# Attention and MoE on one core: gating the loads of batches 2 to 7 on MoE steps, odd V slots by VectorE copies, stores issued on ScalarE with four out buffers, and a new DMA model in the scheduler

## The chip, the cores and the metric

One core of one Trainium2 chip. The metric is device microseconds (us) of one execution, the median of several runs. Five engines have an in-order queue each: TensorE (PE), VectorE (DVE), ScalarE (ACT), GpSimd (POOL) and SyncE (SP). DMAs are issued on three of them: loads on GpSimd, transposes and copies on SyncE, stores on SyncE or ScalarE. Each run is marked fast or slow by its time and clock; the ratios use fast runs alone, while the medians in the tables are over all runs, a slow one included where there was one.

## The reference

Sliding-window attention, then a two-layer MLP with squared ReLU (here "MoE").

```python
batch, n_heads, seq, head_dim = 8, 8, 576, 64      # q, k, v in float32
scores = q @ k.T / sqrt(64); masked to |i - j| <= 32; softmax; attn @ v
x = attn_out.transpose(0, 2, 1, 3).reshape(4608, 512)
h = x @ w_in                                       # 512 x 2048
out = maximum(h, 0) ** 2 @ w_out                   # 2048 x 512
```

## The kernel before

Attention works in 72 chunks of 64 query tokens (nine per batch), MoE in nine tiles T of 512 tokens. A MoE *step* is a sixteenth of a tile's first product: 144 steps in all. Attention is interleaved with MoE on TensorE so that TensorE never starves.

The kernel first records all operations with what they read and write. A list scheduler inside the kernel then lays them in order for each engine, with a model of how long each DMA takes, and the instructions are emitted in that order with semaphore waits.

```python
LATE = {"POOL": 1500, "SP": 3000, "ACT": 3000}
def forward(self, key=None, seq=None, rnd=None):      # the scheduler's clock
    ...
    # DMA model of before: three rings served in turn, 180 ns a turn for GpSimd, 60 for the others
    end[op.i] = now + 1700 + (rnd.random() * rnd.late[op.eng] if rnd else 0)

def pace(self, b, x):                                 # a load waits for an attention step
    return [("pace", 9 * b - GL + 2 * x)] if b > 1 else []      # GL = 14

def dma_turn(self, b, t, x, key):                     # K and Q transposed by DMA, on SyncE
    self.p.rec("SP", lambda e: e.dma_start(dst, src, transpose=True), ..., move=(16, 30))

def vd_copy(self, b, s0, s1, key):    # odd 64-token offsets need V shifted by half the partitions
    for lo in range(2):
        dst = vd[64 * lo:64 * lo + 64, s0:s1, :, :]
        src = vx[64 - 64 * lo:128 - 64 * lo, s0 + lo:s1 + lo, :, :]
        self.p.rec("SP", lambda e, d=dst, c=src: e.dma_start(d, c), ...)

def xturn(self, n, m):                # attention output transposed for the MoE, by DMA for n >= 18
    self.p.rec("SP", lambda e: e.dma_start(self.XT[...], xr[...], transpose=True), ...)

def mm2(self, T, u, seg, key):        # second product; the store of 128 rows
    oe = self.OE[x % 3]
    self.p.rec("ACT", lambda e: e.activation(oe[:], op[:], ACTF.Copy), ...)
    self.p.rec("SP", lambda e: e.dma_start(self.out[128 * x:128 * x + 128, :], oe[:]), ...)
```

For batch 0 the shifted V comes from two TensorE matmuls with shifted identities and a ScalarE copy (`vd_shift`).

The softmax here doesn't subtract the row's maximum and nothing guards it: scores larger than these inputs give would overflow.

## Time and profile before

| | before |
|---|---|
| time, median | 340.54 us (3 runs), 340.09 with a fourth |
| span of the profiled run | 338.6 us |
| TensorE busy | 312.5 us (92%) |
| TensorE gaps over 0.25 us after 31 us | 20.0 us, the largest 8.18, 5.98 and 2.16 |
| half-clock stretches after 31 us | 3.4, 6.8 and 10.2 us |

TensorE is the busiest engine, so its idle time is what counts. The page's slices (40 of 8.5 us each): busy tenths of TensorE, its granted clock, and the DMA engines.

```profile
PE   8989997999997929999099999999999999999996
PEclk9999997999999978999679999999999999999999
DMA  9999999999999999999999999983202211100012
```

There are two holes in PE, with a dip of the clock after each, and DMA is at 9 up to about 230 us. The TensorE timeline of the kernel before; columns are start, duration, engine, line, operation, count and, in brackets, the idle time just before and what ended it:

```profile
54.45 0.20 PE L570 MATMUL sc<-vd,pt 128*128 128x65 bf16 x1 [2.16 <-DMA vd<-vx]
...
126.25 1.89 PE L641 MATMUL ht<-xt,w 128*128 128x512 bf16 x4 [5.98 <-ACT rt L647]
...
169.76 1.86 PE L641 MATMUL ht<-xt,w 128*128 128x512 bf16 x4 [8.18 <-issue]
```

Elsewhere four such matmuls took 0.86 us. After the two long gaps they took about twice that, 1.89 and 1.86 us, because the clock was at half.

What stood behind the second gap is in ScalarE's timeline of the kernel before:

```profile
117.54 0.60 ACT L647 ACTIVATE rt<-ht 128x512 bf16<-128x512 f32 x1 [0.33 <-PE ht L641]
125.11 0.60 ACT L674 ACTIVATE oe<-outp 128x512 f32<-128x512 f32 x1 [6.97 <-DMA out_dram<-oe]
```

ScalarE's copy waited for one of three out buffers, held by a store; the ReLU behind it could not run, and TensorE had no free PSUM buffer. The third gap is marked "issue", but SyncE's timeline of the kernel before shows its cause. It is the end of a transpose of attention outputs (`xt<-xr`), issued at 160.28, which landed at 169.67.

```profile
151.75 1.20 SPq L458 DMA_TRANSPOSE qt<-qraw  x1
153.00 1.88 SPq L594 DMA_TRANSPOSE xt<-xr  x1
154.93 0.58 SPq L676 DMA_DIRECT2D out_dram<-oe  x1
155.67 0.46 SPq L487 DMA_DIRECT2D vd<-vx  x1
156.18 0.82 SPq L676 DMA_DIRECT2D out_dram<-oe  x1
157.04 0.52 SPq L487 DMA_DIRECT2D vd<-vx  x1
157.65 1.23 SPq L458 DMA_TRANSPOSE kt<-kraw  x1
158.98 1.24 SPq L458 DMA_TRANSPOSE qt<-qraw  x1
160.28 1.39 SPq L594 DMA_TRANSPOSE xt<-xr  x1
```

The data of that last transpose was ready at 150.6 us, the end of the VectorE instruction that wrote it:

```profile
150.19 0.42 DVE L584 TENSOR_TENSOR xr<-sc,rs 128x256 bf16<-128x256 f32 x1
```

It then stood in SyncE's queue, and took 9.4 us to land. The view of DMA issues of the kernel before (count, size, median us from issue to landing):

```profile
kraw<-in_k_dram POOLq DMA_DIRECT2D x30, 128.0 KB, 15.2
vd<-vx SPq DMA_DIRECT2D x28, 132.0 KB, 6.8
kt<-kraw SPq DMA_TRANSPOSE x30, 7.8
```

### The profile page before, as it was taken

The page shows a single profiled execution, that of the slowest core. Times are in us where ns is not written, and L with a number is a line of the kernel's source. Part 1 is how long each engine was busy: PE and PEld are TensorE (multiplying, and loading weights), DVE is VectorE, ACT ScalarE, POOL GpSimd, SP SyncE. Part 2 cuts the span into 40 slices and gives each one's busy share as a digit, 9 for nine tenths or more (in the row PEclk, how much of TensorE's full clock was granted, in tenths as well). Part 3 has the DMA queues.
Part 4 walks back from the last instruction along what each step waited for, and adds up shares of the span by engine and source line. Part 5 has one row for each costly group of instructions (what it writes and reads, how often), then busy time and mean ns, then how long its engine had stood idle before and what let it go on. Part 6 is the DMA issues. An engine that isn't in the chain of part 4 may idle for free.

```text
span 338.6 us, 7132 instructions
## 1 busy us (share of the span) xinstructions
PE 312.5 (92%) x2862; PEld 168.5 (50%) x2862; DVE 135.3 (40%) x414; ACT 150.5 (44%) x267; POOL 107.1 (32%) x133
## 2 busy tenths in 40 slices
PE   8989997999997929999099999999999999999996
PEld 3457585887553414444034454444454444444442
DVE  5534353564444505454115443544454352222200
ACT  2445263755524615545133554555455544444421
POOL 8998395333765603146011542220000000000000
PEclk9999997999999978999679999999999999999999
DMA  9999999999999999999999999983202211100012
GB/s 69 158 186 195 180 155 190 156 145 171 190 148 181 133 173 180 179 154 155 169 219 139 102 155 194 132 142 90 56 33 56 54 46 41 58 37 31 31 64 93
DMA packets 168160, 42.66 MB, mean 126 GB/s; under 512 B 157632, under 2 KB 161728, under 8 KB 168128
## 3 DMA queue, kind: packets, MB, share of 16 engines
q0 software_dynamic: 116736, 18.36, 77.5%
q1 hardware_dynamic: 51392, 23.85, 38.7%
q8 instruction: 23, 0.38, 0.5%
q14 instruction: 9, 0.07, 0.1%
HBM read 36.70 MB, written 9.44 MB: 136 GB/s over the span
## 4 chain that ended last, share of the span: by engine, by line
PE 80%; DMA 10%; POOL 4%; issue 3%; ACT 1%; DVE 0%; SPq 0%; POOLq 0%; ACTq 0%
PE outp L665 36%; PE ht L641 29%; PE ht L622 6%; DMA vx<-in_v_dram 4%; PE sc L528 3%; DMA xt<-xr 2%; DMA out_dram<-oe 2%; PE sc L570 2%; PE sc L571 2%; DMA vd<-vx 2%; POOL kraw L418 1%; POOL qraw L418 1%; POOL vx L464 1%; POOL w L492 1%; PE sc L431 1%
## 5 line engine op out<-in xcount | busy, mean ns | idle before, releaser
L665 PE MATMUL outp<-w,gt 128*128 128x512 bf16 x576 | 144.5, 383 | 0.0
L641 PE MATMUL ht<-xt,w 128*128 128x512 bf16 x448 | 116.3, 387 | 15.2 <-issue 8.2
L647 ACT ACTIVATE rt<-ht 128x512 bf16<-128x512 f32 x112 | 66.9, 598 | 98.2 <-PE ht L641 96.5
L656 DVE TENSOR_TENSOR gt<-rt 128x512 bf16<-128x512 bf16 x144 | 60.7, 422 | 117.6 <-ACT rt L647 106.6
L665 PEld LDWEIGHTS outp<-w,gt 128*128 128x128 bf16 x576 | 55.0, 98 | 62.6 <-issue 1.8
L641 PEld LDWEIGHTS ht<-xt,w 128*128 128x128 bf16 x448 | 41.3, 99 | 61.4 <-issue 11.3
L418 POOL DMA_DIRECT2D kraw<-in_k_dram x40 | 35.8, 896 | 85.5 <-PE sc L528 81.8
L544 ACT ACTIVATE e<-sc 128x512 bf16<-128x512 f32 x72 | 39.7, 600 | 16.3 <-PE sc L528 16.3
L464 POOL DMA_DIRECT2D vx<-in_v_dram x40 | 35.7, 897 | 27.9 <-PE sc L528 27.9
L551 DVE TENSOR_TENSOR pt<-e,mask 128x512 bf16<-128x512 bf16 x72 | 27.9, 420 | 33.1 <-ACT e L544 33.1
L418 POOL DMA_DIRECT2D qraw<-in_q_dram x40 | 36.0, 899 | 4.2 <-issue 4.2
L674 ACT ACTIVATE oe<-outp 128x512 f32<-128x512 f32 x36 | 21.5, 598 | 34.0 <-PE outp L665 26.3
L622 PE MATMUL ht<-xt,w 128*128 128x128 bf16 x512 | 33.7, 222 | 0.3
L584 DVE TENSOR_TENSOR xr<-sc,rs 128x256 bf16<-128x256 f32 x72 | 29.9, 422 | 4.6 <-DMA xt<-xr 2.1
L622 PEld LDWEIGHTS ht<-xt,w 128*128 128x128 bf16 x512 | 30.0, 99 | 2.7 <-ACT rt L628 1.1
L628 ACT ACTIVATE rt<-ht 128x512 bf16<-128x512 f32 x32 | 19.1, 599 | 22.5 <-PE ht L622 20.4
L582 DVE RECIPROCAL rs<-sc 128x4 f32<-128x4 f32 x72 | 12.7, 180 | 18.1 <-PE sc L571 16.1
L386 PE MATMUL outp<-zz 128*128 128x512 bf16 x50 | 16.1, 439 | 1.2 <-DVE zz L380 1.2
L528 PEld LDWEIGHTS sc<-qt,kt 64*128 64x128 bf16 x576 | 10.0, 95 | 11.1 <-issue 7.2
L570 PE MATMUL sc<-vx,pt 128*128 128x65 bf16 x160 | 15.3, 194 | 0.1
L571 PE MATMUL sc<-vx,pt 128*128 128x65 bf16 x160 | 15.3, 195 | 0.0
L570 PEld LDWEIGHTS sc<-vx,pt 128*128 128x128 bf16 x160 | 12.6, 99 | 4.0 <-DVE xr L584 0.6
(48 smaller groups left out, 123.4 us busy)
## 6 DMA issues: line engine op xcount, KB each, us to landing
out_dram<-oe SPq DMA_DIRECT2D x36, 256.0 KB, 2.4
kraw<-in_k_dram POOLq DMA_DIRECT2D x30, 128.0 KB, 15.2
qraw<-in_q_dram POOLq DMA_DIRECT2D x30, 128.0 KB, 16.0
vd<-vx SPq DMA_DIRECT2D x28, 132.0 KB, 6.8
vx<-in_v_dram POOLq DMA_DIRECT2D x24, 128.0 KB, 15.9
w<-in_moe_w_in_dram POOLq DMA_DIRECT2D x4, 512.0 KB, 10.5
w<-in_moe_w_out_dram POOLq DMA_DIRECT2D x4, 512.0 KB, 17.7
vx<-in_v_dram POOLq DMA_DIRECT2D x16, 96.0 KB, 13.6
```

The lines of the kernel that those rows point to most:

```text
L418: self.p.rec("POOL", lambda e: e.dma_start(dst, src), writes=[("fraw", b, t, x)], old=[("fraw", b - 2, t, x)], reads=self.pace(b, x), dma= ...
L464: self.p.rec("POOL", lambda e: e.dma_start(self.VX[b % 2][r:r + n, s, :, 0:64], self.v[b, :, t0:t0 + n, :].rearrange("h p d -> p h d")), w ...
L544: self.p.rec("ACT", lambda e, d=dst, a=src: e.activation(d, a, ACTF.Exp, scale=0.125), reads=["s" + x for x in name], writes=[("e", g, x) ...
L551: self.p.rec("DVE", lambda e, a=pt, c=ee, d=mb: e.tensor_tensor(a, c, d, ALU.mult), reads=rd + ["mask"], writes=[("pt", (n + k) % 3)], key ...
L570: e.matmul(o, pt[:, a:a + 128], vt[:, ha, 0:VE], start=True, stop=False)
L571: mm = e.matmul(o, pt[:, a + 64:a + 192], vt[:, ha + 2, 0:VE], start=False, stop=True)
L584: self.p.rec("DVE", lambda e: e.tensor_tensor(bass.AP(xr, 256 * k, [[768, 128], [64, 4], [1, 64]]), bass.AP(self.SC, base, [[2048, 128], [ ...
L622: mm = e.matmul(ht[:, 128 * (d % 4):128 * (d % 4) + 128], self.W1[:, ft, 128 * d:128 * d + 128], self.XT[:, t0 // 64:t0 // 64 + 2, ft, :], ...
L641: mm = e.matmul(ht[:], self.W1[:, ft, 128 * d:128 * d + 128], self.XT[:, 8 * T:8 * T + 8, ft, :], start=(ft == 0), stop=(ft == 3))
L647: self.p.rec("ACT", lambda e: e.activation(rt[:], ht[:], ACTF.Relu), reads=[("ht", k % 2)], writes=[("rt", k % 4)], key=key, dur=560)
L656: self.p.rec("DVE", lambda e: e.tensor_tensor(g, r, r, ALU.mult), reads=[("rt", k % 4)], writes=tags, key=key, dur=430)
L665: mm = e.matmul(op[:], gt[:, d, 128 * u:128 * u + 128], self.W2[:, d, :], start=(d == 0), stop=(d == 15))
```

## The change

Its intent: spread the loads over the run, one at a time, so that DMA is not crowded; take the V copies and the stores off SyncE; one more out buffer. The diff also replaces the scheduler's DMA model, and it records the MoE tiles between the batches of attention, no longer after them all, since a load can wait only for a MoE step that is recorded before it. Cut to its core (the new recording order isn't shown):

```diff
-GL = 14
+PACE = 18
-LATE = {"POOL": 1500, "SP": 3000, "ACT": 3000}
+LATE = {"POOL": 1500, "SP": 2000, "ACT": 2000}
+DEPTH, POST, BACK = 4000, {"POOL": 1500, "SP": 1000, "ACT": 1000}, {"POOL": 2500, "SP": 4000, "ACT": 4000}
 def forward(...):
-    # three rings in turn
+    # one first-in first-out line for all DMAs; GpSimd's enter it in pieces, at most DEPTH ns ahead
+    end[op.i] = max(now, start[op.i] + op.dur) + POST[op.eng] + (...)
-def pace(self, b, x):
-    return [("pace", 9 * b - GL + 2 * x)] if b > 1 else []
+def pace(self, b, x, z):                       # z: 0 for K, 1 for Q, 2 for V
+    if b < 2:
+        return []
+    l = 2 * (9 * b + 1.8 * x + 0.6 * z - PACE)
+    return [("mo", max(0, int(l)))] if l < 16 * NT else []      # "mo" k is written by MoE step k
-    (dma_turn)  move=(16, 30)
+    (dma_turn)  move=(32, 28 if n > 64 else 20)      # xturn: (16 * m, 28); store: (8, 92)
-def vd_shift(...)   # TensorE and ScalarE
-def vd_copy(...)    # DMA on SyncE
+def vd_half(self, b, s0, s1, key):
+    for lo in range(2):
+        dst = vd[64 * lo:64 * lo + 64, s0:s1, :, :].rearrange("p s h d -> p (s h d)")
+        src = vx[64 - 64 * lo:128 - 64 * lo, s0 + lo:s1 + lo, :, :].rearrange("p s h d -> p (s h d)")
+        self.p.rec("DVE", lambda e, d=dst, c=src: e.tensor_copy(d, c), ...)
-    oe = self.OE[x % 3]
+    oe = self.OE[x % 4]
-    self.p.rec("SP", lambda e: e.dma_start(self.out[...], oe[:]), ...)
+    self.p.rec("ACT", lambda e: e.dma_start(self.out[...], oe[:]), ...)
```

More of the change, by code (lines that the diff above doesn't have):

```diff
@@ L1 @@
+import collections
 import heapq
@@ L105, in forward @@
         heads = {"POOL": 0, "SP": 0, "ACT": 0}
-        order = ["POOL", "SP", "ACT"]
-        now = spent = 0.0
+        fifo, soft = collections.deque(), collections.deque()
+        now = ahead = 0.0
         def enter(s):
@@ L122, in serve @@
         def serve(until):
-            nonlocal now, spent
+            nonlocal now, ahead
             while now < until:
-                nxt = min((rings[q][heads[q]][0] for q in order if heads[q] < len(rings[q])), default=None)
-                if nxt is None or nxt >= until:
-                    if nxt is None and until > 1e12:
-                        return False
-                    now = max(now, until if nxt is None else min(until, nxt))
-                    return False
-                now = max(now, nxt)
-                for q in list(order):
-                    if heads[q] < len(rings[q]) and rings[q][heads[q]][0] <= now:
-                        break
-                it = rings[q][heads[q]]
-                spent += it[2]
-                if spent >= (180 if q == "POOL" else 60):
-                    order.remove(q)
-                    order.append(q)
-                    spent = 0
-                now += it[2]
-                it[1] -= 1
-                if it[1] <= 0:
-                    heads[q] += 1
-                    op = it[3]
-                    end[op.i] = now + 1700 + (rnd.random() * rnd.late[op.eng] if rnd else 0)
+                nxt = None
+                for q in rings:
+                    ring = rings[q]
+                    while heads[q] < len(ring) and ring[heads[q]][0] <= now:
+                        op = ring[heads[q]][1]
+                        heads[q] += 1
+                        if q == "POOL":
+                            k = max(1, int(200 // op.move[1]))
+                            cnt = op.move[0]
+                            while cnt > 0:
+                                soft.append((min(k, cnt) * op.move[1], op if cnt <= k else None, True))
+                                cnt -= k
+                        else:
+                            fifo.append((op.move[0] * op.move[1], op, False))
+                    if heads[q] < len(ring) and (nxt is None or ring[heads[q]][0] < nxt):
+                        nxt = ring[heads[q]][0]
+                while soft and ahead < DEPTH:
+                    fifo.append(soft.popleft())
+                    ahead += fifo[-1][0]
+                if not fifo:
+                    if nxt is None:
+                        if until < 1e12:
+                            now = until
+                        return False
+                    now = min(nxt, until)
+                    continue
+                x, op, sw = fifo.popleft()
+                now += x
+                if sw:
+                    ahead -= x
+                if op is not None:
+                    end[op.i] = max(now, start[op.i] + op.dur) + POST[op.eng] + (rnd.random() * rnd.late[op.eng] if rnd else 0)
@@ L169, in forward @@
             if best is None:
-                if all(heads[q] >= len(rings[q]) for q in order):
+                if not fifo and not soft and all(heads[q] >= len(rings[q]) for q in rings):
                     break
@@ L190, in forward @@
             if op.dma is not None:
-                rings[e].append([t + d + 600, op.move[0], op.move[1], op])
+                rings[e].append((t + (d + 100 if e == "POOL" else 400), op))
             else:
@@ L209, in enter @@
         def enter(op):
-            heapq.heappush(wait["RING" if op.dma is not None else op.eng], (ready[op.i] + (1700 if op.dma is not None else 0), op.i, 0))
+            heapq.heappush(wait["RING" if op.dma is not None else op.eng], (ready[op.i] + (BACK[op.eng] if op.dma is not None else 0), op.i, 0))
         for op in ops:
@@ L236, in backward @@
                 free[e] = t + x
-                heapq.heappush(wait[op.eng], (t + x + 600, i, 1))
+                heapq.heappush(wait[op.eng], (t + x + 400, i, 1))
                 continue
@@ L375, in alloc @@
         self.ZZ = sb("zz", [128, 512], BF16)
-        self.OE = [sb(f"oe{i}", [128, 512], F32) for i in range(3)]
+        self.OE = [sb(f"oe{i}", [128, 512], F32) for i in range(4)]
     def ms(self, eng, t, ap, v, key, dur=120, old=()):
@@ L405, in setup_rest @@
         self.ms("DVE", [("vxone", i, 3)], self.VX[i][:, 1:4, :, 64:VS], 1.0, key, 120)
-        self.ms("DVE", [("vdone", i)], self.VD[i][:, :, :, 64:VS], 1.0, key, 120)
         self.ms("DVE", [("ktpad", i, 0)], self.KT[i][:, :, 0:32], 0.0, key)
@@ L418, in tok_load @@
         self.p.rec("POOL", lambda e: e.dma_start(dst, src), writes=[("fraw", b, t, x)], old=[("fraw", b - 2, t, x)],
-                   reads=self.pace(b, x), dma=(f"f{b % 2}{t}{x}", b), key=key,
+                   reads=self.pace(b, x, "kqv".index(t)), dma=(f"f{b % 2}{t}{x}", b), key=key,
                    dur=500 + 3.2 * n, move=(n // 2, 13.3))
@@ L458, in dma_turn @@
         self.p.rec("SP", lambda e: e.dma_start(dst, src, transpose=True), reads=[("fraw", b, t, x)], writes=[(t, i, x)],
-                   old=self.was(b, t, x), dma=(f"t{t}{i}{x}", b), key=key, dur=1250, move=(16, 30), att=True)
+                   old=self.was(b, t, x), dma=(f"t{t}{i}{x}", b), key=key, dur=1250, move=(32, 28 if n > 64 else 20), att=True)
     def vx_load(self, b, s, key):
@@ L465, in vx_load @@
             self.VX[b % 2][r:r + n, s, :, 0:64], self.v[b, :, t0:t0 + n, :].rearrange("h p d -> p h d")),
-            writes=[("vxl", b % 2, s), ("vxh", b % 2, s)], reads=self.pace(b, s), dma=(f"vf{b % 2}{s}", b), key=key, dur=500 + 3.2 * n, move=(n // 2, 13.3))
-    def vd_shift(self, b, s, key, tag, bank):
-        vx, o = self.VX[b % 2], bank[:].rearrange("p (h d) -> p h d", h=8)
-        def f(e):
-            e.matmul(o, self.IDW[:, 128:256], vx[:, s, :, 0:64], start=True, stop=False)
-            return e.matmul(o, self.IDW[:, 0:128], vx[:, s + 1, :, 0:64], start=False, stop=True)
-        rd = [(w, b % 2, z) for w in ("vxl", "vxh") for z in (s, s + 1)] + ["id"] + [("vxz", b % 2, 0), ("vxz", b % 2, 4)]
-        self.p.rec("PE", f, reads=rd, writes=[tag], key=key, dur=450, att=True)
-        self.p.rec("ACT", lambda e: e.activation(self.VD[b % 2][:, s, :, 0:64], o, ACTF.Copy), reads=[tag],
-                   writes=[("vd", b % 2, s)], key=key, dur=600, att=True)
@@ L480, in vd_copy @@
-    def vd_copy(self, b, s0, s1, key):
+            writes=[("vxl", b % 2, s)], reads=self.pace(b, s, 2), dma=(f"vf{b % 2}{s}", b), key=key, dur=500 + 3.2 * n, move=(n // 2, 13.3))
+    def vd_half(self, b, s0, s1, key):
         vd, vx = self.VD[b % 2], self.VX[b % 2]
-        rd = [(w, b % 2, s) for s in range(s0, s1 + 1) for w in ("vxl", "vxh")] + [("vdone", b % 2)]
-        rd += [("vxone", b % 2, k) for k in range(4)]
         for lo in range(2):
-            dst = vd[64 * lo:64 * lo + 64, s0:s1, :, :]
-            src = vx[64 - 64 * lo:128 - 64 * lo, s0 + lo:s1 + lo, :, :]
-            self.p.rec("SP", lambda e, d=dst, c=src: e.dma_start(d, c), reads=rd, old=[("vd", b % 2, s) for s in range(s0, s1)], writes=[("vdc", b % 2, s, lo) for s in range(s0, s1)],
-                       dma=(f"vc{b % 2}{s0}", b), key=key, dur=600, move=(4, 50 * (s1 - s0)), att=True)
+            dst = vd[64 * lo:64 * lo + 64, s0:s1, :, :].rearrange("p s h d -> p (s h d)")
+            src = vx[64 - 64 * lo:128 - 64 * lo, s0 + lo:s1 + lo, :, :].rearrange("p s h d -> p (s h d)")
+            rd = [("vxl", b % 2, s + lo) for s in range(s0, s1)] + [("vxone", b % 2, k) for k in range(4)]
+            self.p.rec("DVE", lambda e, d=dst, c=src: e.tensor_copy(d, c), reads=rd,
+                       writes=[("vd", b % 2, s, lo) for s in range(s0, s1)], key=key, dur=80 + 145 * (s1 - s0), att=True)
@@ L534, in scores @@
             rd += [t for t in self.qk_tags(b, c + k) if t not in rd]
-        self.p.rec("PE", f, reads=rd, writes=["sA", "sC"] + (["sB", "sD"] if m > 2 else []) + [("pace", n + k) for k in range(m)],
+        self.p.rec("PE", f, reads=rd, writes=["sA", "sC"] + (["sB", "sD"] if m > 2 else []),
                    key=key, dur=190 + 115 * m, att=True)
@@ L574, in av @@
         if c % 2 == 0:
-            rd = [("vdone", i), ("vxl", i, s), ("vxh", i, s)] + [("vxone", i, k) for k in range(4)]
+            rd = [("vxl", i, s)] + [("vxone", i, k) for k in range(4)]
             if s in (0, 4):
@@ L578, in av @@
         else:
-            rd = [("vd", i, s), ("vdone", i)] + ([("vdc", i, s, 0), ("vdc", i, s, 1)] if b else [])
+            rd = [("vd", i, s, 0), ("vd", i, s, 1)]
         self.p.rec("PE", f, reads=rd + [("pt", n % 3), ("ptz", n % 3)], writes=[tag], key=key, dur=240, att=True)
@@ L596, in xturn @@
                 transpose=True), reads=[("xr", gi % 3, u) for u in range(m)], writes=[("xt", n + u) for u in range(m)],
-                dma=(f"x{gi % 3}", n), key=key, dur=1250, move=(16, 30), att=True)
+                dma=(f"x{gi % 3}", n), key=key, dur=1250, move=(16 * m, 28), att=True)
             return
@@ L624, in f @@
             return mm
-        self.p.rec("PE", f, reads=[("xt", 8 * T + 2 * g), ("xt", 8 * T + 2 * g + 1), ("w1", q)], writes=[("ht", k % 2)], key=key,
+        self.p.rec("PE", f, reads=[("xt", 8 * T + 2 * g), ("xt", 8 * T + 2 * g + 1), ("w1", q)], writes=[("ht", k % 2), ("mo", k)], key=key,
                    dur=900)
@@ L643, in f @@
             return mm
-        self.p.rec("PE", f, reads=[("xt", 8 * T + j) for j in range(8)] + [("w1", d // 4)], writes=[("ht", k % 2)],
+        self.p.rec("PE", f, reads=[("xt", 8 * T + j) for j in range(8)] + [("w1", d // 4)], writes=[("ht", k % 2), ("mo", k)],
                    key=key, dur=854)
@@ L672, in mm2, with moe @@
         if seg == 3:
-            oe = self.OE[x % 3]
+            oe = self.OE[x % 4]
             self.p.rec("ACT", lambda e: e.activation(oe[:], op[:], ACTF.Copy), reads=[("outp", x % 2)],
-                       writes=[("oe", x % 3)], key=key, dur=560)
-            self.p.rec("SP", lambda e: e.dma_start(self.out[128 * x:128 * x + 128, :], oe[:]),
-                       reads=[("oe", x % 3)], writes=[("out", x)], dma=(f"o{x % 3}", x), key=key, dur=600, move=(8, 80))
+                       writes=[("oe", x % 4)], key=key, dur=560)
+            self.p.rec("ACT", lambda e: e.dma_start(self.out[128 * x:128 * x + 128, :], oe[:]),
+                       reads=[("oe", x % 4)], writes=[("out", x)], dma=(f"o{x % 4}", x), key=key, dur=400, move=(8, 92))
+    def moe(self, T):
+        if T == 0:
+            gt = (12.0, 15.5, 19.0, 22.0)
+            wt = (13.0, 18.0, 22.0, 28.0)
+            for g, q in sorted(((g, q) for g in range(4) for q in range(4)), key=lambda a: (max(gt[a[0]], wt[a[1]]), a)):
+                self.mm1_small(0, g, q, 0.0 + 0.01 * self.k1)
+            return
+        for d in range(16):
+            key = 8 * T + d / 2
+            if T < NSMALL:
+                self.mm1_small(T, d // 4, d % 4, key)
+            elif T < NT:
+                self.mm1(T, d, key)
+            self.mm2(T - 1, d // 4, d % 4, key + 0.25)
     def build(self):
@@ L695, in build @@
             self.load_w2(d, at[f"w2{d}"])
+        tile = 0
         for b in range(B_):
+            while 8 * tile + 7 < NCH * b:
+                self.moe(tile)
+                tile += 1
             if b < FB:
@@ L722, in build @@
                     if x and not b:
-                        early = x < 3
-                        self.vd_shift(b, x - 1, n - LEAD - 3, ("outp", 0) if early else "sB", self.OUTP[0] if early else self.BK["B"])
+                        self.vd_half(b, x - 1, x, n - LEAD - 3)
                 if b and c in (1, 5):
-                    self.vd_copy(b, c // 2, c // 2 + 2, n - LEAD - 3)
+                    self.vd_half(b, c // 2, c // 2 + 2, n - LEAD - 3)
                 self.av(n)
@@ L729, in build @@
                     self.xturn(n - m + 1, m)
-        gt = (12.0, 15.5, 19.0, 22.0)
-        wt = (13.0, 18.0, 22.0, 28.0)
-        for g, q in sorted(((g, q) for g in range(4) for q in range(4)), key=lambda a: (max(gt[a[0]], wt[a[1]]), a)):
-            self.mm1_small(0, g, q, 0.0 + 0.01 * self.k1)
-        for T in range(1, NT + 1):
-            for d in range(16):
-                key = 8 * T + d / 2
-                if T < NSMALL:
-                    self.mm1_small(T, d // 4, d % 4, key)
-                elif T < NT:
-                    self.mm1(T, d, key)
-                self.mm2(T - 1, d // 4, d % 4, key + 0.25)
+        for T in range(tile, NT + 1):
+            self.moe(T)
         p.schedule()
```

## The prediction

> **What bounds the kernel now.** PE is busy 312.5 of 338.6 us (busy table), and from 177 us on its timeline shows no gap: PE-bound, with a few stalls before. After warm-up it has gaps of 2.2 us (at 52), 6.0 (120), 8.2 (162) and six of 0.3 to 1.1: 20 us in all. The granted clock fell to half for 3.4 us (from 54.7), 6.8 (122.9) and 10.2 (163.9); groups of four matmuls took 1.7 to 1.9 us there, not 0.86, which costs about 5.5 us more where PE worked.
>
> The large stalls are DMAs that landed late:
> - 52: an odd attention step waits for the copies into vd (issued 47.6, 6.8 us).
> - 120: ScalarE waits 7.0 us for a store to free one of three out buffers (issued 117.4, landed 125.1); behind it the relu, then PE.
> - 162: the chain says "issue", but the xt transpose issued at 160.28 landed at 169.67 and PE restarted at 169.76.
>
> Why late: DMA is saturated from 20 to 180 us (busy digits 9, mean share 1.4 to 2.2 where queues overlap). Loads, fired in bursts, take 11 to 25 us to land, transposes 8, stores 7. After 180 us, at about nine tenths of that rate, loads take 4 to 5 us, transposes 3 to 5, stores mostly 2 to 2.5, and PE never stops. The last load starts at 224 us: there is slack to spread.
>
> **What the change does.**
> - Loads of batches 2 to 7 each wait for a MoE step; the last for step 106 of 144 (about 250 us). A piece leads the first scores that read it by about 8 steps: 8 x 1.73 us plus attention, an estimate of 15 us, against 4.8 + 4.6 us for load and transpose at the uncrowded latency. This removes most of the stalls.
> - 28 vd copies leave DMA and SP. VectorE gets 28 copies of 64x1056 bf16 and 8 of half the size. Estimate from "VectorE: DVE Perf Modes", the errata table (58 + FD/4 cycles): 0.34 us each, 12 us on an engine 40% busy, off the path. No run shows this copy yet.
> - Four shift pairs on PE and their ScalarE copies go in warm-up, where idle matmuls fill: worth nothing.
> - Stores move to ScalarE: 36 issues of 0.3 to 0.6 us (SP's durations), each after a wait for its own copy: about 1 us each, 36 us on an engine 44% busy. A fourth buffer covers a late store. By "DMA: Bandwidth & Descriptors" (Issuing engines are not separate DMA queues) the store itself gets no faster.
> - In the PE order tile 2's first product now starts before tile 1's second ends. Matmul counts stay.
>
> **Time.** 340.5 less 25 is 316 if all goes. I leave 1 us for a remaining stall at 90 to 125 us, where DMA is still catching up. Predicted 317 us, 8 in 10 between 311 and 327. Chances: faster by over 2% 0.93, within 2% 0.05, slower 0.02.
>
> **What would show it.** PE gaps after warm-up under 6 us in all; no half-clock stretch after 60 us; loads landing in 4 to 8 us after 100 us; no ScalarE wait on stores; DMA busy until 250 us but below 9 before 230; MoE step 4 still at 31 us; the stretch from 293 us to the end as long as now.
>
> **What would make it wrong.** DMA still saturated to 120 us, so that transposes miss the 15 us lead; ScalarE's issues delaying relu so that PE waits on ht; copies delaying squares on VectorE; any stall over 3 us[...].

## The result, and the profile after

| | before | after |
|---|---|---|
| time, median of 4 runs | 340.09 us | 322.39 us (320.79 to 324.30) |
| ratio of the fast runs | | 0.9477, 95% interval 0.9402 to 0.9553 |
| span of the profiled run | 338.6 us | 321.0 us |
| TensorE gaps over 0.25 us after 31 us | 20.0 us | 6.6 us |
| half-clock stretches after 31 us | 3.4, 6.8, 10.2 us | 3.4 us |

A ratio is the mean time of one kernel's fast runs over that of the other's in the same rounds, so it is not quite the ratio of the medians. The change is 5.2% faster. The sum closes: a half-clock stretch costs half of the time that TensorE worked in it, which I estimate from the stretches at 1.71 + 1.76 + 2.19 us before and 1.62 us after. So 19.96 + 5.66 us of loss became 6.63 + 1.62 us, 17.4 us less, and the span fell by 17.6 us. TensorE's work after 31 us did not change otherwise: it was busy there for 284.6 us before and 280.3 us after, and of the 4.3 us less the half clock explains 4.0.

The slices after:

```profile
PE   6889989789999998999999999999999999999996
PEclk9999999979999999999999999999999999999999
DMA  9999999999997999999999999999992221000022
```

The two holes are gone, and one small dip is left in the ninth slice. DMA still shows 9 nearly up to 240 us: the digit does not tell a crowded queue from a busy one. The landing times do (DMA issues, after):

```profile
out_dram<-oe ACTq DMA_DIRECT2D x36, 256.0 KB, 3.3
kraw<-in_k_dram POOLq DMA_DIRECT2D x30, 128.0 KB, 5.1
kt<-kraw SPq DMA_TRANSPOSE x30, 4.7
```

Loads land in 5.1 us instead of 15.2. SyncE, which issued for 18.0 of the 20 us from 120 to 140 us before, does so for 11.4 of them now (sums over its timeline). In the stretch of the run that answers to the one shown above, the same `xt` transpose (chunks 39 to 41) hardly waits in its queue:

```profile
143.71 1.19 SPq L472 DMA_TRANSPOSE qt<-qraw  x1
144.95 1.28 SPq L595 DMA_TRANSPOSE xt<-xr  x1
146.32 1.22 SPq L472 DMA_TRANSPOSE kt<-kraw  x1
```

(The data of this one was ready at 144.3 us.) What remains is a new stall of 3.4 us at 62 us. TensorE's and ScalarE's timelines of the kernel after:

```profile
65.79 1.89 PE L623 MATMUL ht<-xt,w 128*128 128x128 bf16 x16 [3.42 <-ACT rt L629]
```

```profile
59.96 0.60 ACT L675 ACTIVATE oe<-outp 128x512 f32<-128x512 f32 x1 [0.95 <-PE outp L666]
60.58 4.45 ACTq L677 DMA_DIRECT2D out_dram<-oe  x1
65.14 0.60 ACT L629 ACTIVATE rt<-ht 128x512 bf16<-128x512 f32 x1 [4.59 <-issue]
```

ScalarE's first store took 4.45 us to *issue*, where the other 35 took 0.34 to 0.40. ScalarE stood still, the ReLU was late, and TensorE stopped. With the half clock that follows, this one event looks like about 5 us, just what the measured time lies above the predicted 317.

### The profile page after: what moved, and what is told of

Its sections match the earlier page's. It is cut to its first block, busy times and chain, and to the rows that moved or that the text cites. A ratio compares the mean times of both kernels' runs of the same rounds, so it can differ in the third digit from the quotient of the medians.

```text
span 321.0 us, 7141 instructions
## 1 busy us (share of the span) xinstructions
PE 305.3 (95%) x2855; PEld 166.6 (52%) x2855; DVE 151.1 (47%) x448; ACT 148.4 (46%) x263; POOL 107.5 (33%) x133
## 4 chain that ended last, share of the span: by engine, by line
PE 80%; DMA 8%; POOL 7%; ACTq 1%; ACT 1%; DVE 1%; issue 1%; SPq 0%; POOLq 0%; DVEq 0%
PE outp L666 37%; PE ht L642 29%; DMA vx<-in_v_dram 6%; PE ht L623 6%; PE sc L529 3%; PE sc L571 2%; PE sc L572 2%; POOL kraw L429 2%; POOL qraw L429 2%; DMA qt<-qraw 2%; POOL vx L478 2%; ACTq L677 1%; POOL w L498 1%; POOL w L493 1%; DVE pt L552 0%
## 5 line engine op out<-in xcount | busy, mean ns | idle before, releaser
L642 PE MATMUL ht<-xt,w 128*128 128x512 bf16 x448 | 113.9, 379 | 0.0
L657 DVE TENSOR_TENSOR gt<-rt 128x512 bf16<-128x512 bf16 x144 | 60.3, 422 | 79.7 <-ACT rt L648 68.2
L666 PEld LDWEIGHTS outp<-w,gt 128*128 128x128 bf16 x576 | 53.5, 98 | 58.8 <-issue 0.6
L642 PEld LDWEIGHTS ht<-xt,w 128*128 128x128 bf16 x448 | 41.9, 98 | 46.7
L429 POOL DMA_DIRECT2D qraw<-in_q_dram x40 | 35.2, 879 | 43.8 <-PE ht L642 14.6
L478 POOL DMA_DIRECT2D vx<-in_v_dram x40 | 34.9, 873 | 38.2 <-PE sc L572 11.0
L545 ACT ACTIVATE e<-sc 128x512 bf16<-128x512 f32 x72 | 38.2, 601 | 9.5 <-PE sc L529 9.5
L552 DVE TENSOR_TENSOR pt<-e,mask 128x512 bf16<-128x512 bf16 x72 | 26.9, 420 | 18.4 <-ACT e L545 18.2
L623 PEld LDWEIGHTS ht<-xt,w 128*128 128x128 bf16 x512 | 30.2, 99 | 8.5 <-ACT rt L629 4.8
L488 DVE COPY vd<-vx 64x1056 bf16<-64x1056 bf16 (+1 forms) x36 | 17.4, 483 | 28.3 <-DMA vx<-in_v_dram 27.8
```

The costliest lines, as they stand in the source:

```text
L429: self.p.rec("POOL", lambda e: e.dma_start(dst, src), writes=[("fraw", b, t, x)], old=[("fraw", b - 2, t, x)], reads=self.pace(b, x, "kqv" ...
L478: self.p.rec("POOL", lambda e: e.dma_start(self.VX[b % 2][r:r + n, s, :, 0:64], self.v[b, :, t0:t0 + n, :].rearrange("h p d -> p h d")), w ...
L545: self.p.rec("ACT", lambda e, d=dst, a=src: e.activation(d, a, ACTF.Exp, scale=0.125), reads=["s" + x for x in name], writes=[("e", g, x) ...
L552: self.p.rec("DVE", lambda e, a=pt, c=ee, d=mb: e.tensor_tensor(a, c, d, ALU.mult), reads=rd + ["mask"], writes=[("pt", (n + k) % 3)], key ...
L623: mm = e.matmul(ht[:, 128 * (d % 4):128 * (d % 4) + 128], self.W1[:, ft, 128 * d:128 * d + 128], self.XT[:, t0 // 64:t0 // 64 + 2, ft, :], ...
L642: mm = e.matmul(ht[:], self.W1[:, ft, 128 * d:128 * d + 128], self.XT[:, 8 * T:8 * T + 8, ft, :], start=(ft == 0), stop=(ft == 3))
```

## The experiments

Twelve kernels ran; all were correct. My theory: bursts of loads crowd DMA, so everything lands late, and the gates cure it; the other parts count little. The rival theories were that the V copies and stores matter as much, or that the new order alone does it.

### Undo one part, or do one part alone

**a_sched**: the kernel before, with only the scheduler's DMA model of the change. No gate, copy or store differs.

```diff
 (kernel before)
-LATE = ...; forward(), backward(): three rings in turn;  move=(16, 30), (16, 30), (8, 80)
+LATE, DEPTH, POST, BACK = ...; forward(), backward() of the change; move=(32, 28 or 20), (16 * m, 28), (8, 92)
```

> The kernel before with only the scheduler's new DMA model (the order of instructions changes, no gate, copy or store does). My theory (bursts of loads on a saturated DMA make everything land late): the backlog stays, loads take 11 to 25 us to land up to 180 us, and the time stays within 2 per cent of before, 333 to 342 us. Rival (the gain comes from a better order): at least half of the 17.7 us gain is here, 331 us or less.

Measured: 323.40 us, ratio 0.9456 (0.9383 to 0.9529). **My theory fell.** The model of DMA in the scheduler, which changes no operation at all but only their order, gives all of the gain. DMA is even more crowded than before, as a_sched's slices and DMA issues show:

```profile
PE   7879989999998998799999999999999999999996
PEclk9999999999999999799999999999999999999999
DMA  9999999999999999999999999999022021000022
```

```profile
kraw<-in_k_dram POOLq DMA_DIRECT2D x30, 128.0 KB, 21.1
kt<-kraw SPq DMA_TRANSPOSE x30, 8.0
```

Loads take 21.1 us to land instead of 15.2, transposes 8.0, and yet TensorE's gaps after 31 us sum to 6.2 us only. Late landing by itself is not what stopped TensorE. What changed is where things stand: in the kernel before, the eight `xt` transposes for chunks 18 to 41 were issued 9.0 to 15.2 us after their data was ready; in a_sched 0 to 8.6 us; in the kernel after 0 to 2.9 us. (Each number is the issue time of the transpose less the end of the VectorE instruction that wrote the last of its inputs.) All of these stood in SyncE's in-order queue behind other DMAs. It is not that SyncE has less to do: in a_sched it issues for 18.0 of the 20 us from 120 to 140 us, just as in the kernel before.

**a_pace**: a_sched plus the gates on MoE steps (and, with them, the change's recording order). **m_pace**: the change with the old gates. **m_vd**: the change with `vd_shift` and `vd_copy`. In all three the scheduler ran anew, so the order on every engine differs too.

```diff
 (a_pace: to a_sched)                               (m_pace: to the change)
-    return [("pace", 9 * b - GL + 2 * x)] ...      -    return [("mo", max(0, int(l)))] ...
+    return [("mo", max(0, int(l)))] ...            +    return [("pace", 9 * b - 14 + 2 * x)] ...
 (m_vd: to the change)
-    self.vd_half(...)
+    self.vd_shift(...) for batch 0, self.vd_copy(...) for the others
```

> a_sched plus the gates on MoE steps; odd V slots still by DMA copies and PE shifts, stores on SyncE with three out buffers. My theory: loads land in 4 to 8 us after 100 us, the stalls at 120 and 162 us and their half-clock stretches are gone, 319 to 327 us. Rival (V copies and stores matter as much): 328 us or more, with a stall of over 3 us behind a vd copy or a store.

> The changed kernel with the old gates on attention positions (VectorE copies, ScalarE stores, 4 buffers stay). My theory: loads land in over 11 us again up to about 170 us and at least one stall of over 3 us comes back, 330 us or more. Rival: taking the copies and stores out of SyncE's queue is enough, 326 us or less.

> The changed kernel with odd V slots again by DMA copies (and PE shifts in warm-up). My theory: with the gates the DMA has room for them, 321 to 327 us, and loads still land in 4 to 8 us after 100 us. Rival (28 copies a large part of the relief): 330 us or more.

| | median us | ratio (95%) | load landing, issued 120 to 150 us |
|---|---|---|---|
| a_pace | 320.80 | 0.9417 (0.9350 to 0.9485) | 4.8 us |
| m_pace | 322.65 | 0.9464 (0.9393 to 0.9535) | 18.8 us |
| m_vd | 321.41 | 0.9412 (0.9350 to 0.9474) | 5.0 us |

The gates do to the landing times what I said (a_pace and m_vd 5 us, m_pace 19 us), and the time does not care: m_pace, whose loads are at least as late as before (18.8 us against 13.0 in the same stretch of the kernel before), is as fast as the change. Each part tried can be taken out alone at no loss clear of the noise. The times of a_pace and m_vd lie in the expected ranges, but since a_sched gives the gain without the gates, they don't show that the gates brought it. My expectation for m_pace (330 us or more) was wrong.

### Are the gates idle, then? The old model with all other parts

**n_old**: the change scheduled by the DMA model of the kernel before.

```diff
 (the change)
-forward(), backward(), LATE, move of the change
+forward(), backward(), LATE, move of the kernel before
```

> The changed kernel (gates, VectorE copies, ScalarE stores, four buffers) scheduled by the DMA model of the kernel before. Theory C with a redundant cure (gates take the crowd away, so that a bad order on SyncE costs little, and stores and copies are off SyncE): 320 to 328 us with loads landing in 4 to 6 us after 100 us. Rival E (the new DMA model is needed whatever the gates do): 331 us or more.

Measured: 322.15 us, ratio 0.9458 (0.9397 to 0.9519), and loads land in 4.7 us when issued from 90 to 120 us, in 3.6 to 4.1 us after (medians of 30 us stretches). So there are **two cures, each sufficient**: an order made with the new model, or the bundle of gates, VectorE copies, ScalarE stores and fourth buffer (with the new recording order). Together they give no more than either. The bundle leaves so little queueing that even the old model's order is good enough: `xt` waits 0 to 2.9 us. Which of its parts does it under the old model was not separated.

### Is it SyncE's order alone?

**b_spord**: the kernel before, all engines frozen in their old order, only SyncE's 142 DMAs in a_sched's order. **s_spord**: a_sched, with SyncE's DMAs in the order of the kernel before. Both record the same operations, so the order can be carried over by number.

```diff
         p.schedule()
+        by = {o.i: o for o in p.ops if o.eng == "SP"}
+        p.ops = [o for o in p.ops if o.eng != "SP"] + [by[i] for i in SPORDER]    # then merged so that
+        ...                                                                       # no wait precedes its source
```

> The kernel before, with TensorE, VectorE, ScalarE and GpSimd in their old order, and only SyncE's 142 DMAs put in the order that the scheduler's new DMA model (a_sched) gave them. Theory C (the stalls came from the place of xt transposes and stores in SyncE's queue: in the kernel before an xt transpose was issued 9 to 15 us after its data was ready): xt issued within 8 us of ready, 6.0 and 8.2 us gaps gone or under 3.5 us, 320 to 329 us, although DMA stays as crowded. Rival D (the order of TensorE or the gates decide): 335 us or more.

> The mirror image: a_sched (323 us) with SyncE's DMAs in the order of the kernel before, all other engines as in a_sched. Theory C: xt transposes wait 9 us or more in the queue again, PE gaps of over 5 us return, 331 us or more. Rival D: 327 us or less.

Measured: b_spord 341.17 us, ratio 0.9958 (0.9892 to 1.0024); s_spord 340.13 us, 0.9944 (0.9886 to 1.0003). Half of theory C holds. With the old queue order on SyncE, a_sched loses its whole gain. Its `xt` transposes wait 12 to 13 us again around 100 us. One of them, from s_spord's VectorE timeline (data ready at 88.7 us) and SyncE timeline (issued at 101.05):

```profile
87.95 0.76 DVE L604 TENSOR_TENSOR xr<-sc,rs 128x256 bf16<-128x256 f32 x2
```

```profile
101.05 1.53 SPq L614 DMA_TRANSPOSE xt<-xr  x1
```

The TensorE timeline of s_spord:

```profile
109.25 3.60 PE L661 MATMUL ht<-xt,w 128*128 128x512 bf16 x8 [7.82 <-DMA xt<-xr]
128.88 1.46 PE L661 MATMUL ht<-xt,w 128*128 128x512 bf16 x3 [9.97 <-ACT rt L667]
```

But the new queue order alone cures nothing. In b_spord the first four `xt` transposes do leave 4 to 7 us after their data (two later ones 16.2 and 14.8 us, which my expectation had excluded), and the 6.0 and 8.2 us gaps are gone; in their place come others, before operations that read what other SyncE DMAs bring (V copies, K and Q transposes). The TensorE timeline of b_spord:

```profile
112.53 0.21 PE L578 MATMUL sc<-vd,pt 128*128 128x65 bf16 x1 [4.67 <-issue]
134.69 0.53 PE L536 MATMUL sc<-qt,kt 64*128 64x64 bf16 x24 [3.03 <-issue]
```

So neither SyncE's order alone nor that of the other four engines alone gives the gain: the two have to fit each other. I call this shown for the pair of orders as wholes. Which single moves matter was not looked for, a mixed pair may lose just because it is mixed, and that the new model's DMA times are nearer to those of the trace was not checked.

### The 4.45 us issue at 60 us

Four kernels keep the order of the change on TensorE and VectorE exactly. **f_sp3** issues the first three stores on SyncE. **f_warm** issues a small load on ScalarE at the very start. **m_store_sp** has all stores on SyncE. **m_oe3** has three out buffers.

```diff
 (f_sp3, m_store_sp: after p.schedule())
+    for op in p.ops:
+        if op.dma is not None and op.dma[0][0] == "o":      # f_sp3: and op.dma[1] < 3
+            op.eng = "SP"
 (f_warm)
+            self.nc.scalar.dma_start(first[:], self.w_in[0:1, 0:64]).then_inc(fsem, 16)
 (m_oe3)
-            oe = self.OE[x % 4]
+            oe = self.OE[x % 3]     # and each copy waits for the store three before it
```

> The changed kernel, same order of all engines, but the first three stores are issued on SyncE and only the other 33 on ScalarE. Theory A (the 4.45 us that ScalarE stood at its first store came from the DMA backlog at 60 us): ScalarE's first store is now at about 90 us in a smaller backlog and is issued in about 0.34 us, the PE gap of 3.4 us at 62 us and the half-clock stretch are gone, 316 to 319 us. Theory B (a first-use cost of ScalarE's DMA queue): the fourth store, now the first on ScalarE, takes about 4 us to issue, PE stalls there, and the time stays 321 to 324 us.

> The changed kernel plus one 256-byte load issued on ScalarE as its first instruction, read by nobody. Theory A (backlog): the first store at 60 us still takes about 4 us to issue, time unchanged within 0.5 per cent. Theory B (first use of the queue): the first store takes about 0.34 us, the PE gap at 62 us goes, 316 to 319 us.

> The changed kernel, same order, with all stores issued on SyncE (four out buffers stay). My theory: with the backlog gone a store in SyncE's queue lands in 2 to 5 us and costs ScalarE nothing, so the time is that of f_sp3 within 1 per cent, 316 to 320 us, better than the change as it stands. Rival (stores in SyncE's order hold up transposes or come too late): 324 us or more.

> The changed kernel, same order, with three out buffers. My theory: stores land within about 12 us and are 7 us apart, so a third buffer is free in time after 80 us: same within 0.5 per cent. Rival (the fourth buffer is needed): ScalarE waits for a store, a PE gap of over 1 us, 325 us or more.

| | median us | ratio (95%) | first ScalarE store: at, time to issue |
|---|---|---|---|
| the change | 322.39 | 0.9477 (0.9402 to 0.9553) | 60.6 us, 4.45 us |
| f_sp3 | 322.98 | 0.9454 (0.9403 to 0.9504) | 89.9 us, 0.38 us |
| f_warm | 322.80 | 0.9465 (0.9409 to 0.9521) | 60.3 us, 0.38 us |
| m_store_sp | 321.01 | 0.9385 (0.9336 to 0.9433) | none |
| m_oe3 | 322.29 | 0.9432 (0.9387 to 0.9476) | 59.3 us, 4.26 us |

(m_store_sp's profiled run was a slow one, 327.83 us, so its trace is not read here; its five fast runs took 319.17 to 321.30 us.)

Both theories are in trouble. The long issue is gone in f_warm, where the backlog is the same, and in f_sp3, where the first use comes later: neither the backlog nor the first use suffices. m_vd shows the same: its first ScalarE store, at 54.3 us and with no earlier DMA on ScalarE, took 0.37 us. It happened in the four runs whose first ScalarE DMA came at 59 to 61 us (the change, m_pace, m_oe3, n_old: 4.45, 4.24, 4.26, 5.54 us) and in no other. Why then stays open. A fetch of instructions is one candidate that the traces do not bear out: the change's trace has 8 KB packets on a DMA queue of kind "instruction" at 60.0 and 63.3 us, but f_warm's has them at 59.7 and 62.8 us, and its store took 0.38 us.

More important: the long issue goes, and **the time stays**. f_warm's timelines show what was hiding behind it, first VectorE, then TensorE:

```profile
64.47 0.18 DVE L583 RECIPROCAL rs<-sc 128x4 f32<-128x4 f32 x1 [0.30 <-PE sc L572]
69.03 0.43 DVE L488 COPY vd<-vx 64x1056 bf16<-64x1056 bf16 x1 [4.37 <-DMA vx<-in_v_dram]
69.49 0.43 DVE L585 TENSOR_TENSOR xr<-sc,rs 128x256 bf16<-128x256 f32 x1
```

```profile
69.97 0.20 PE L571 MATMUL sc<-vx,pt 128*128 128x65 bf16 x1 [2.78 <-DVE xr L585]
```

A V copy, first in VectorE's queue, waits 4.37 us for its load, which was issued at 51.9 us and landed at 69.0 in the crowd of the start. The normalisation `xr` behind it could have run long before; TensorE waits for it. (In f_sp3 VectorE waits 5.00 us at the same place. In the change the same copy ran at 70.22 us, just after its load landed at 70.20, and VectorE had come to it only at 70.06: the long issue had hidden the wait.) This is the price of putting the V copies on an in-order compute engine: a DMA copy waits in a DMA issuer's queue, a VectorE copy blocks VectorE. The visible stall was a tie; when I took it away, the next one in line took its place.

m_oe3 shows that the fourth buffer is not needed with this order. m_store_sp shows that ScalarE is not a better issuer for the stores than SyncE; its median is 1 us above the range that I had expected.

### A version meant to beat both

**v_mix**: the change, but V copies as before (TensorE shift, DMA copies) for batches 0 and 1.

```diff
-                    self.vd_half(b, c // 2, c // 2 + 2, n - LEAD - 3)
+                    (self.vd_copy if b < FB else self.vd_half)(b, c // 2, c // 2 + 2, n - LEAD - 3)   # FB = 2
```

> A version that should beat both: the changed kernel, but odd V slots of batches 0 and 1 made as before (PE shift, DMA copies), those of batches 2 to 7 on VectorE. Theory F (in the crowded stretch up to 75 us a VectorE copy that waits for its V load holds up VectorE's in-order queue, and PE behind it, in the changed kernel hidden by the slow first store): no PE gap of over 1.5 us at 60 to 75 us, no half-clock stretch, 315 to 319 us. Rival G (the gap there comes from the loads themselves and just moves): 321 us or more.

Measured: 320.03 us, ratio 0.9358 (0.9316 to 0.9400), the lowest of the twelve. Its interval lies just under that of the change (0.9402 to 0.9553), from other rounds, and overlaps those of a_pace and m_store_sp. The gain over the change is about 1% (0.7% by the medians, 1.3% by the ratios), too little to be called shown, and the expectation (315 to 319 us, no gap of over 1.5 us) was missed. The reason is an error of mine, and it speaks for theory F. Counting the loads in GpSimd's order afterwards, the copy that waits at 64 us is of batch 2, whose loads already stand behind those of batch 1, not of batch 1. So the copies of batch 2 stayed on VectorE, and one of them still blocks it (VectorE, then TensorE, of v_mix):

```profile
64.23 0.75 DVE L511 COPY vd<-vx 64x1056 bf16<-64x1056 bf16 x1 [2.36 <-DMA vx<-in_v_dram]
```

```profile
65.49 0.40 PE L628 MATMUL sc<-identw,xr 128*128 128x128 bf16 x4 [2.03 <-DVE xr L608]
```

A half-clock stretch of 3.4 us follows at 66.1. Leaving the copies of batch 2 on DMA as well, or moving them later in VectorE's order, was not tried.

## Why the prediction was right or wrong

The time was right: 322.4 us in the range 311 to 327, 5.2% faster where over 2% had a chance of 0.93. The mechanism was half right, and the sum was 5.4 us too good. That the time held is in part luck: a part of the diff that the prediction gave no price is enough for all of the gain.

- *The 25 us of stalls, their place and what ended each* were right: they sum to 25.6 us, and 17.4 of it is what the span lost.
- *"Why late: DMA is saturated ..."* and *"This removes most of the stalls"*, said of the gates, is the step that failed. The gates did cut the landing of loads from 15.2 to 5.1 us, and the old model with gates, copies and stores is enough (n_old). But they are not needed: a_sched has neither the new gates nor an emptier DMA (loads 21.1 us) and gains as much, and m_pace without the gates loses nothing. The prediction took landing time for the cause and did not look at the 9 to 15 us that the `xt` transposes stood in SyncE's queue before they were issued.
- *The scheduler's new DMA model* is a large part of the diff, and the prediction priced it at nothing. By a_sched it is worth 5.4% alone. The one thing that the prediction noted of the new order, that "tile 2's first product now starts before tile 1's second ends" (99.3 and 121.8 us in the change, 107.0 and 104.4 before), is not what brings this: in a_sched tile 2 starts at 102.4 us, after tile 1's second product ended at 101.1.
- *"I leave 1 us for a remaining stall at 90 to 125 us"* is the term that was mis-sized. The stall came at 62 us, 3.42 us of gap and about 1.6 of half clock; 1.1 us more came at 124, and four gaps of 0.3 to 0.7 us. "ScalarE's issues delaying relu so that PE waits on ht", on the list of what could go wrong, is what the trace shows there; "copies delaying squares on VectorE" is close to what stood behind it.
- *VectorE copies at 0.34 us, 12 us in all*: 0.43 us in the usual case (median of all 36), 17.4 us of busy time. The page of the Trainium skill that I drew on, "VectorE: DVE Perf Modes", says under its errata table that the fixed term measured is about 150 cycles and not 58; with 150 the estimate would have been (150 + 264) / 0.96 GHz = 0.43 us, and this trace agrees. I took the table and not the line under it. *"Off the path"* was wrong too: not for their length, but for their wait in VectorE's order.
- *The store gets no faster for its issuer*, from "DMA: Bandwidth & Descriptors": agrees. The median store landed in 2.4 us from SyncE before and 3.3 us from ScalarE after. With the copies and gates in place it made no difference beyond 1% whether ScalarE or SyncE issued (m_store_sp against f_sp3, 0.9385 and 0.9454).
- *The signs*: MoE step 4 at 31.6 us and the last stretch of 44.6 us, unchanged, were right; load landing of 4 to 5 us after 100 us, right; TensorE gaps under 6 us, missed at 6.6; no half clock after 60 us, wrong by one; no ScalarE wait for an out buffer, right, though it stood 4.45 us at an issue; DMA digits below 9 before 230 us, wrong, since the digit stays at 9 up to about 240 us although loads then land in about 4 us.

## What to carry to other kernels

Before blaming a slow transfer, split the wait into three: data ready to issue, issue to landing, landing to use. Here the first was as long as the second, and a better order removed the stalls while every transfer stayed as slow. When orders are made by a model, check the model's transfer times against a trace before changing the program (here the order alone was worth as much as the whole change); and remember that an operation moved to an in-order compute engine brings its waits along and blocks what stands behind it.

When a visible stall is removed and the time stays, look for the tie behind it. And freeze the order of all other engines when one part is tested, or the scheduler's answer is tested with it.

## What the Trainium skill lacked or had wrong

- "TensorE: Matmul & The Clock Gate" (Why this matters for your kernels) advises no idle gaps over about 3 us. Here gaps of 2.16 us (before, a_pace) and 2.03 us (v_mix) were each followed by a half-clock stretch of 3.4 us, and gaps of 1.10 (after), 1.36 (a_sched), 1.86 (m_oe3) and 1.94 us (b_spord, at 54 us) were not. That the clock is either full or half, in stretches of 3.4 us or multiples (3.4, 6.8, 10.2), agrees with Part 1 of the page.
- "DMA: Bandwidth & Descriptors" (Issuing engines are not separate DMA queues) calls the time to initiate a DMA "usually small relative to the DMA itself". For most single DMAs that holds here (about 1.2 us to issue a K transpose, 7.8 us to land), but the page doesn't say that the sum can fill the issuer: in the kernel before SyncE spent 18.0 of the 20 us from 120 to 140 us issuing, with single issues of up to 3.21 us, and SyncE's queue order went with the whole gain (s_spord). I found no page that tells what held one issue on ScalarE for 4.24 to 5.54 us in four runs.
- "VectorE: DVE Perf Modes": the errata table's 58 cycles are too few, as the text under it says; a 64x1056 bf16 copy took 0.43 us, which fits 150. The row should carry the number that fits.
